# Moving q0's load, the output weights and the first mixer of an attention and token-mixer kernel

## The chip, the cores and the metric

The kernel runs on one core of one Trainium2 chip. The core has five engines with queues of their own: TensorE (PE, whose weight loads are listed as PEld), VectorE (DVE), ScalarE (ACT), GpSimd (POOL) and SyncE (SP). Each executes its instructions in the order of the program and waits where a semaphore says so. The metric is device time in microseconds (us) for one execution; lower is better. The profile is one execution taken by the hardware profiler.

## The reference

There are 4 batches, 8 heads, 768 positions and a head size of 64, in f32. The first half is a causal linear attention with a decay per head; the second mixes the tokens of each batch.

```
for each block of 64 positions:
    intra = (qb @ kb.T * lam**(i - j) for i >= j) @ vb
    inter = (qb * lam**(i + 1)) @ state
    out   = intra + inter
    state = lam**64 * state + (kb * lam**(63 - i)).T @ vb
x  = out as [4, 768, 512]
wq = x @ w_q          # 512 -> 64
wk = x @ w_k
W  = (wq @ wk.T) / 8
y  = relu(W @ x) @ w_out   # 512 -> 512
```

The kernel need not follow the blocks of 64: it uses chunks of 128, and it regroups W @ x as wq @ (wk.T @ x), which needs no matrix of 768 by 768.

## The kernel before, in words

**Tiling.** Two heads make a pair, so that their 2 x 64 columns fill 128 partitions. There are 16 pairs, four a batch, and the main loop has one step for each pair: step n, with n from 0 to 15 (`for n in range(N)`, L553). Lambda's powers are folded into q (`Dq`, multiplied in at L234) and v (`DvI`, multiplied in by `scale_v`, L198), so scores need only a 0/1 mask.

**Loads.** For each pair q, k and v are read as f32 and cast to bf16 on the way, by DMAs that GpSimd issues (`load_q` L81, `load_kv` L86; 196 KB written each). Pair 0 is different: k and q come as f32 by SP (L101, L103) and are cast on chip (L525 to L533). GpSimd's queue holds, in one order, its constants, all these loads, the scaling of v from pair 4 on, and the weights: `wqk` (L190) and `wo`, the 512 by 512 output weights, which step 3 issues (L557). A dictionary `pool` (L545) lists what GpSimd does in steps 0 to 5; from step 6 on `load_more(n + 5)` does.

**One step on PE, in order.** `scores(n)` (12 matmuls), `inter(n-1)`, `values(n-1)`, `flip(n-2)` (transposes of the attention output into `xT`), the outputs of the list `outs`, `turn_q(n+1)` and `turn_k(n+1)` (transposes of the next q and k), `states(n)`, then the outputs of `late_outs`. DVE multiplies the scores by the mask in four pieces a step (`masks`, L320), multiplies the transposed q by Dq, copies `xT` and sums the states; ACT copies k (L252), the attention output (L361) and the output products (L515).

**The mixer of a batch** comes in parts: `mix_wk` (x @ w_k), `mix_wq` (x @ w_q), `mix_py` (wk.T @ x, and its three copies into Y, of which the last two put the halves' partitions the other way round), `mix_pm` (Y with wq, then ReLU into `rmT`; dd numbers the four blocks of 128 columns, each in two halves of 384 positions), and `mix_po` (rmT @ wo for 128 positions, a copy, and a store). In the second half of the kernel one batch's mixer runs within the attention steps of the next. `mix_py` stands at the end of steps 5, 9 and 13, `mix_pm` at the head of steps 7 and 8 (batch 0), 11 and 12 (batch 1), 15 and after the loop.

**What sets the order.** The order is written out by hand; nothing reorders it. [...] Stores wait: at step 9 SP issues a dummy copy (`late`, L573) that waits for the load of v of pair 14, and only then the stores.

Of the kernel before, what the change touches and what calls it, by code (L numbers as in the profile page):

```python
# [10 lines left out]
BF16 = mybir.dt.bfloat16  # L11
F32 = mybir.dt.float32
ALU = mybir.AluOpType
ACT = mybir.ActivationFunctionType

B, H, S, D = 4, 8, 768, 64
CH = 128
# [11 lines left out]
def kernel(  # L29
# [28 lines left out]
    def pst(shape, dt, name):  # L58
        i = free.pop(0)
        t = ps.tile(shape, dt, tag=f"p{i}", name=name)  # L60
        held[id(t)] = (t, i)
        return t

    def done(t):
        free.append(held.pop(id(t))[1])
# [7 lines left out]
    def q_rows(n):  # L73
        b, kk = pairs[n]
        return q[b, 2 * kk : 2 * kk + 2].rearrange("h (a p r) d -> p h a (r d)", p=128, r=2)
# [10 lines left out]
    def load_kv(n, nm):  # L86
        t = stage.tile([128, 2, NCH, D], BF16, tag="f" + nm, name="f" + nm)
        nc.gpsimd.dma_start(out=t, in_=kv_rows(n, dict(k=k, v=v)[nm]))  # L88
        staged[n, nm] = t

    def load(n):
        load_q(n)
        load_kv(n, "k")
        load_kv(n, "v")


    load_kv(0, "v")
    lam1 = consts.tile([1, H], F32, name="lam1")
    nc.sync.dma_start(out=lam1, in_=lam.rearrange("(o h) -> o h", o=1))
    k0 = consts.tile([128, 2, NCH, D], F32, name="k0")  # L100
    nc.sync.dma_start(out=k0, in_=kv_rows(0, k))  # L101
    q0 = consts.tile([128, 2, 3, 2 * D], F32, name="q0")
    nc.sync.dma_start(out=q0, in_=q_rows(0))  # L103


    nc.scalar.preload_act_table_set("natural_log_exp_and_others")
# [3 lines left out]
    nc.vector.memset(blank, 0.0)  # L110
    ident = consts.tile([128, 128], BF16, name="ident")
    nc.vector.memset(ident, 0.0)
    maskc = consts.tile([128, 3, CH], BF16, name="maskc")
    nc.vector.memset(maskc, 1.0)
    nc.gpsimd.affine_select(
# [13 lines left out]
        channel_multiplier=1,  # L129
        allow_small_or_imprecise_dtypes=True,  # L130
    )
    ET = consts.tile([128, S], F32, name="ET")
    nc.gpsimd.iota(
        ET,
        pattern=[[128, NCH], [1, 2], [2, 64]],
        base=1,
        channel_multiplier=0,
        allow_small_or_imprecise_dtypes=True,
    )
    load(1)  # L140
    nc.gpsimd.affine_select(
        out=maskc.rearrange("j c (r p) -> j c r p", r=2),
        in_=maskc.rearrange("j c (r p) -> j c r p", r=2),
# [19 lines left out]
    lnl = consts.tile([128, H], F32, name="lnl")  # L163
    nc.scalar.activation(out=lnl, in_=lam_all, func=ACT.Ln)
    done(lam_all)
    pw48 = consts.tile([128, H, NCH], F32, name="pw48")
    nc.vector.tensor_tensor(
        out=pw48,
# [1 line left out]
        in1=lnl.unsqueeze(2).to_broadcast([128, H, NCH]),  # L170
        op=ALU.mult,
    )
    lnv = lnl.rearrange("p (k l) -> p k l", l=2)
    lncol = consts.tile([128, NP], F32, name="lncol")
    for hl in range(2):
        nc.vector.tensor_copy(
            out=lncol[hl * 64 : hl * 64 + 64, :], in_=lnv[hl * 64 : hl * 64 + 64, :, hl]
        )
    Dq = [consts.tile([128, S], BF16, name=f"dq{kk}") for kk in range(NP)]

    def make_dq(kk):
        nc.scalar.activation(out=Dq[kk], in_=ET, func=ACT.Exp, scale=lncol[:, kk : kk + 1])

    DvI = consts.tile([128, H, NCH], F32, name="DvI")
    nc.scalar.activation(out=DvI, in_=pw48, func=ACT.Exp, scale=-1.0)

    wqk = consts.tile([128, 2, 4, DHY], BF16, name="wqk")
    wo = consts.tile([128, 4, HD], BF16, name="wo")

    def load_wqk():  # L190
        for i, w in ((1, moe_w_k), (0, moe_w_q)):
# [29 lines left out]
    def turn_q(n):  # L221
        b, kk = pairs[n]
        fq = staged.pop((n, "q"))
        trq = pst([128, NCH, 2, 64], BF16, "trq")
        for a in range(3):
            for r in range(2):
                for hl in range(2):
                    nc.tensor.transpose(  # L228
                        trq[hl * 64 : hl * 64 + 64, 2 * a : 2 * a + 2, r, :],
                        fq[:, hl, a, r * D : (r + 1) * D],  # L230
                        ident,
                    )
        qT = tsb.tile([128, S], BF16, tag="qT", name="qT")
        nc.vector.tensor_tensor(  # L234
            out=qT,
            in0=trq.rearrange("d c r p -> d (c r p)"),
            in1=Dq[kk],
            op=ALU.mult,
        )
        done(trq)  # L240
        L[n]["qT"] = qT
# [75 lines left out]
    def masks(n, which):  # L317
        for a, hl in which:
            t = prb.tile([128, 3, CH], BF16, tag="pr", name="pr")
            nc.vector.tensor_tensor(out=t, in0=L[n]["sc"][a, hl], in1=maskc, op=ALU.mult)  # L320
            done(L[n]["sc"][a, hl])
            L[n]["pr"][a, hl] = t
# [175 lines left out]
    def mix_po(b, t, last=False):  # L498
        cols = (256, 256) if last and t == NCH - 1 else (HD,)
        osb = outp.tile([128, HD], F32, tag="osb", name="osb")  # L500
        c = 0
        for w in cols:
            po = pst([128, w], F32, "po")
            for kt in range(4):
                nc.tensor.matmul(  # L505
                    po,
                    M[b]["rmT"][:, kt, t * CH : (t + 1) * CH],
                    wo[:, kt, c : c + w],
                    start=(kt == 0),
                    stop=(kt == 3),  # L510
                )
            if last and (c or (t % 2 and len(cols) == 1)):
                nc.vector.tensor_copy(out=osb[:, c : c + w], in_=po)
            else:
                nc.scalar.copy(out=osb[:, c : c + w], in_=po)  # L515
            done(po)
            stores.append((b, t, c, w, osb))
            c += w
        if b > 0:
            store()  # L520
# [7 lines left out]
    make_dq(0)  # L528
    turn_k(0)
    warm(2)  # L530
    fq0 = nat.tile([128, 2, 3, 2 * D], BF16, tag="q0", name="fq0")
    nc.vector.tensor_copy(out=fq0[:, 0], in_=q0[:, 0])  # L532
    nc.vector.tensor_copy(out=fq0[:, 1], in_=q0[:, 1])  # L533
    staged[0, "q"] = fq0
    turn_q(0)
    warm(2)
    scale_v(0, nc.vector)
# [2 lines left out]
    load_kv(5, "k")  # L540
    load_wqk()
    load_kv(5, "v")


    pool = {  # L545
        0: ["q6", "k6", "s4", "v6"],
        1: ["q7", "k7", "s5", "v7"],
        2: ["q8", "s6", "k8", "v8"],
        3: ["wo"],
        4: ["s7", "q9", "k9"],  # L550
        5: ["s8", "v9", "q10", "k10", "v10"],
    }
    for n in range(N):  # L553
        b, kk = pairs[n]
        for what in pool.get(n, []):
            if what == "wo":
                nc.gpsimd.dma_start(  # L557
                    out=wo, in_=moe_w_out.rearrange("(kt p) j -> p kt j", p=128)
                )
            elif what[0] == "s":  # L560
                scale_v(int(what[1:]), nc.gpsimd)
            elif what[0] == "q":
                load_q(int(what[1:]))
            else:
                load_kv(int(what[1:]), what[0])
        if 11 <= n + 5 < N:
            load_more(n + 5)
        if n + 5 >= N and n + 3 < N:
            scale_v(n + 3, nc.gpsimd)
        if n == 9:  # L570

            late = consts.tile([1, D], BF16, name="late")
            nc.sync.dma_start(out=late, in_=staged[14, "v"][0:1, 0, 0, :])  # L573
            store()
        p = b - 1
        outs = {
            8: [(0, 0), (0, 1)],
            9: [(0, 3)],
            11: [(0, 5)],
            12: [(1, 0)],  # L580
            13: [(1, 2)],
            14: [(1, 3)],
            15: [(1, 5)],
        }.get(n, [])

        late_outs = {8: [(0, 2)], 10: [(0, 4)], 12: [(1, 1)], 14: [(1, 4)]}.get(n, [])

        def back():

            if kk == 1 and n > 8:  # L590
                flip(n - 2, nc.scalar)
            if n >= 1:
                values(n - 1)
            if n >= 2 and not (kk == 1 and n > 8) and n != 5:
                flip(n - 2, nc.scalar if n < 5 else None)
            for i, t in outs:
                mix_po(i, t)
            if kk == 1 and n > 8:
                mix_wk(p)


        if n > 5 and n % 4 in (3, 0):
            mix_pm(
                (n - 5) // 4,
                [0, 1] if n % 4 == 3 else [2, 3],
                engs=(nc.scalar, nc.vector) * 2 if n > 8 else None,
            )
        scores(n)
        if n >= 1:
            inter(n - 1)  # L610
        masks(n, ((0, 0), (0, 1)))
        back()

        if 1 <= n < 3:
            make_dq(n + 1)
        if n in (2, 3):
            scale_v(n, nc.vector)
        masks(n, ((1, 0),))
        if n < N - 1:
            turn_q(n + 1)  # L620
        masks(n, ((1, 1),))
        if n < N - 1:
            turn_k(n + 1)
        states(n)
        if n == 4:
            flip(n - 1)
        for i, t in late_outs:
            mix_po(i, t)
        sums(n)
        if n == 0:  # L630
            scale_v(1, nc.vector)
        if n == 4:
            mix_wk(p, (0, 1, 2))
            mix_wk(p, (3,))
        if n == 5 or kk == 1 and n > 8:
            mix_wq(p)
            mix_py(p)
    bl = B - 1
# [52 lines left out]
```

## Time and profile before

| | us |
|---|---|
| median of 11 runs | 102.16 |
| shortest, longest | 100.14, 105.72 |
| the profiled execution | 105.52 |
| its span, first to last instruction | 103.7 |
| PE busy | 86.0 (83% of the span) |
| DVE, ACT, POOL busy | 68.0, 63.2, 66.0 |
| start of the scores of steps 5 to 9 | 28.23, 32.45, 35.64, 39.34, 51.68 |
| start of the scores of steps 10 to 15 | 57.12, 60.86, 65.38, 70.17, 75.61, 80.21 |

The profiled execution is one of the long ones: 3.4 us above the median of the runs shown. Busy time is the share in which an engine has an instruction in execution; matmuls overlap in a pipeline, so a busy PE is not PE at its best. The timeline lists, for each group of instructions, its start, its length, the engine, the line, what is written and read, and, in brackets, how long the engine was idle just before and what ended that.

### The profile page before, as it was taken

The page shows a single profiled execution, that of the slowest core. Times are in us where ns is not written, and L with a number is a line of the kernel's source. Part 1 is how long each engine was busy: PE and PEld are TensorE (multiplying, and loading weights), DVE is VectorE, ACT ScalarE, POOL GpSimd, SP SyncE. Part 2 cuts the span into 40 slices and gives each one's busy share as a digit, 9 for nine tenths or more (in the row PEclk, how much of TensorE's full clock was granted, in tenths as well). Part 3 has the DMA queues.
Part 4 walks back from the last instruction along what each step waited for, and adds up shares of the span by engine and source line. Part 5 has one row for each costly group of instructions (what it writes and reads, how often), then busy time and mean ns, then how long its engine had stood idle before and what let it go on. Part 6 is the DMA issues. An engine that isn't in the chain of part 4 may idle for free.

```text
span 103.7 us, 3512 instructions
## 1 busy us (share of the span) xinstructions
PE 86.0 (83%) x1497; PEld 57.5 (55%) x1507; DVE 68.0 (66%) x152; ACT 63.2 (61%) x122; POOL 66.0 (64%) x69
## 2 busy tenths in 40 slices
PE   4967678687998998039999999899999989999950
PEld 1415566566887685013778856556966566443430
DVE  3247999797695988300538999995698993246330
ACT  4281487897466989002577876666796775568330
POOL 5999999889989980999999999990500000000000
PEclk9999999999999999855899999999999999999999
DMA  0999999999999999999999999999972221533583
GB/s 20 257 177 156 164 166 165 160 172 154 163 168 163 139 131 159 117 100 151 160 161 150 150 131 154 145 123 299 394 281 103 101 108 58 203 143 132 227 311 140
DMA packets 67440, 16.99 MB, mean 164 GB/s; under 512 B 62946, under 2 KB 64482, under 8 KB 67426
## 3 DMA queue, kind: packets, MB, share of 16 engines
q0 software_dynamic: 61456, 9.70, 127.4%
q1 hardware_dynamic: 5826, 6.95, 18.8%
q8 instruction: 11, 0.18, 0.6%
q10 hardware_dynamic: 144, 0.13, 0.4%
q14 instruction: 3, 0.02, 0.1%
HBM read 20.19 MB, written 6.29 MB: 255 GB/s over the span
## 4 chain that ended last, share of the span: by engine, by line
PE 38%; DMA 25%; POOL 17%; DVE 11%; ACT 3%; issue 3%; POOLq 0%
PE po L505 18%; DMA wo<-in_moe_w_out_dram 11%; DMA fk<-in_k_dram 8%; DMA fv<-in_v_dram 6%; POOL fv L88 5%; POOL fk L88 5%; DVE pr L320 4%; PE trq L228 3%; POOL fq L83 3%; POOL vn L202 3%; PE xp L369 3%; PE oa L349 2%; DVE rmT L477 2%; PE wk L392 2%; PE py L433 2%
## 5 line engine op out<-in xcount | busy, mean ns | idle before, releaser
L320 DVE TENSOR_TENSOR pr<-sc,maskc 128x384 bf16<-128x384 f32 x64 | 33.4, 548 | 2.4 <-PE sc L307 2.1
L505 PE MATMUL po<-wo,rmT 128*128 128x512 bf16 (+1 forms) x90 | 24.4, 390 | 5.0 <-DMA wo<-in_moe_w_out_dram 4.2
L515 ACT COPY osb<-po 128x512 f32<-128x512 f32 (+1 forms) x22 | 12.6, 580 | 15.6 <-PE po L505 15.1
L202 POOL TENSOR_TENSOR vn<-fv,DvI 128x768 bf16<-128x768 bf16 x12 | 17.9, 1492 | 6.0 <-DMA fv<-in_v_dram 3.3
L252 ACT COPY kT<-trk 128x768 bf16<-128x768 bf16 x16 | 12.8, 802 | 8.1 <-PE trk L248 8.1
L88 POOL DMA_DIRECT2D fv<-in_v_dram x16 | 17.1, 1071 | 0.9 <-POOLq L675 0.8
L361 ACT CAST xnat<-oa 128x384 bf16<-128x384 f32 x31 | 13.4, 483 | 6.7 <-PE oa L349 6.6
L505 PEld LDWEIGHTS <-rmT 128*128 128x128 bf16 x100 | 8.9, 101 | 13.9 <-DMA wo<-in_moe_w_out_dram 4.4
L88 POOL DMA_DIRECT2D fk<-in_k_dram x15 | 15.7, 1049 | 0.4 <-DMA fk<-in_k_dram 0.4
L234 DVE TENSOR_TENSOR qT<-trq,dq 128x768 bf16<-128x768 bf16 x16 | 8.8, 552 | 10.7 <-PE trq L228 9.9
L83 POOL DMA_DIRECT2D fq<-in_q_dram x15 | 12.8, 853 | 0.3 <-issue 0.3
L307 PE MATMUL sc<-qT,kT 64*128 64x128 bf16 x192 | 9.5, 217 | 3.5 <-ACT kT L252 2.1
L307 PEld LDWEIGHTS <-kT 64*128 64x128 bf16 x192 | 6.1, 94 | 8.3 <-ACT kT L252 5.3
L228 PE MATMUL trq<-ident,fq 128*64 128x128 bf16 x192 | 9.2, 229 | 1.8 <-DVE fq L532 0.7
L228 PEld LDWEIGHTS <-fq 128*64 128x64 bf16 x192 | 6.3, 113 | 5.5 <-issue 2.9
L486 ACT ACTIVATE rmT<-pm 128x384 bf16<-128x384 f32 x20 | 8.6, 500 | 0.1
L248 PE MATMUL trk<-ident,fk 128*64 128x128 bf16 x180 | 7.8, 223 | 0.7 <-DMA fk<-in_k_dram 0.6
L349 PE MATMUL oa<-vn,pr 128*128 128x64 bf16 x192 | 8.4, 194 | 0.0
L369 PE MATMUL xp<-ident,xnat 128*128 128x128 bf16 x96 | 8.0, 219 | 0.2
L267 PE MATMUL dps<-vn,fk 128*64 128x128 bf16 (+4 forms) x150 | 7.9, 232 | 0.1
L349 PEld LDWEIGHTS <-pr 128*128 128x128 bf16 x192 | 6.6, 98 | 0.7
L267 PEld LDWEIGHTS <-fk 128*64 128x64 bf16 x150 | 6.2, 110 | 1.0 <-DVE xT L377 0.4
(63 smaller groups left out, 111.0 us busy)
## 6 DMA issues: line engine op xcount, KB each, us to landing
out_dram<-osb SPq DMA_DIRECT2D x23, 256.0 KB, 2.1
fv<-in_v_dram POOLq DMA_DIRECT2D x16, 192.0 KB, 6.2
fq<-in_q_dram POOLq DMA_DIRECT2D x15, 192.0 KB, 5.8
fk<-in_k_dram POOLq DMA_DIRECT2D x15, 192.0 KB, 6.2
wo<-in_moe_w_out_dram POOLq DMA_DIRECT2D x1, 512.0 KB, 11.2
k<-in_k_dram SPq DMA_DIRECT2D x1, 384.0 KB, 3.5
q<-in_q_dram SPq DMA_DIRECT2D x1, 384.0 KB, 5.7
out_dram<-osb ACTq DMA_DIRECT2D x1, 128.0 KB, 2.1
```

The costliest lines, as they stand in the source:

```text
L83: nc.gpsimd.dma_start(out=t, in_=q_rows(n))
L88: nc.gpsimd.dma_start(out=t, in_=kv_rows(n, dict(k=k, v=v)[nm]))
L202: eng.tensor_tensor(out=vn, in0=fv, in1=DvI[:, 2 * kk : 2 * kk + 2, :].unsqueeze(3).to_broadcast([128, 2, NCH, D]), op=ALU.mult,)
L228: nc.tensor.transpose(trq[hl * 64 : hl * 64 + 64, 2 * a : 2 * a + 2, r, :], fq[:, hl, a, r * D : (r + 1) * D], ident,)
L252: nc.scalar.copy(out=kT, in_=trk)
L267: nc.tensor.matmul(dps[hl * 64 : hl * 64 + 64, c:end, :], kn[:, hl, c, :], vn[:, hl, c, :].unsqueeze(1).to_broadcast([128, end - c, D]), s ...
L307: nc.tensor.matmul(sc[a, hl][:, cc, :], kT[r, c * CH : (c + 1) * CH], qchunk(n, r, c), start=True, stop=True, skip_group_check=True,)
L320: nc.vector.tensor_tensor(out=t, in0=L[n]["sc"][a, hl], in1=maskc, op=ALU.mult)
L349: nc.tensor.matmul(oa[hl][:, c, :], pr[c // 3, hl][:, c % 3, :], vn[:, hl, c, :], start=False, stop=(c == NCH - 1), skip_group_check=True,)
L361: nc.scalar.copy(out=to, in_=oa[hl])
L505: nc.tensor.matmul(po, M[b]["rmT"][:, kt, t * CH : (t + 1) * CH], wo[:, kt, c : c + w], start=(kt == 0), stop=(kt == 3),)
L515: nc.scalar.copy(out=osb[:, c : c + w], in_=po)
```

## The change

It has five parts. (1) The ramp `ET` is made by a running sum on DVE instead of an iota on GpSimd, in natural order; the Exp that makes Dq reads it with a stride of two elements to get the order it needs. (2) q of pair 0 is loaded by GpSimd as all the others, first in its queue, and q of pair 1 third; SP's f32 load and the two DVE casts go. (3) `wo` is laid out as four blocks of 128 columns, loaded in pieces of 128 columns, and issued behind q and k of pair 6, ahead of the loop; the lists in `pool` are shifted to suit. (4) In step 5 `mix_wq` stands behind `turn_q`, `mix_py` behind `turn_k`, and the first two blocks of `mix_pm` at the end of the step. (5) The other blocks of `mix_pm` come one to a step (`thirds`, at the head of steps 7, 8 and 10 to 15), half by ACT and half by DVE, and the outputs are spread anew over `outs` and `late_outs`.

```diff
@@ -94,13 +94,13 @@
         load_kv(n, "v")
 
 
+    load_q(0)
     load_kv(0, "v")
+    load_q(1)
     lam1 = consts.tile([1, H], F32, name="lam1")
     nc.sync.dma_start(out=lam1, in_=lam.rearrange("(o h) -> o h", o=1))
     k0 = consts.tile([128, 2, NCH, D], F32, name="k0")
     nc.sync.dma_start(out=k0, in_=kv_rows(0, k))
-    q0 = consts.tile([128, 2, 3, 2 * D], F32, name="q0")
-    nc.sync.dma_start(out=q0, in_=q_rows(0))
 
 
     nc.scalar.preload_act_table_set("natural_log_exp_and_others")
@@ -110,6 +110,18 @@
     nc.vector.memset(blank, 0.0)
     ident = consts.tile([128, 128], BF16, name="ident")
     nc.vector.memset(ident, 0.0)
+
+    one = consts.tile([128, 1], F32, name="one")
+    nc.vector.memset(one, 1.0)
+    ET = consts.tile([128, S], F32, name="ET")
+    nc.vector.tensor_tensor_scan(
+        out=ET,
+        data0=one.to_broadcast([128, S]),
+        data1=one.to_broadcast([128, S]),
+        initial=0.0,
+        op0=ALU.mult,
+        op1=ALU.add,
+    )
...
-    ET = consts.tile([128, S], F32, name="ET")
-    nc.gpsimd.iota(
-        ET,
-        pattern=[[128, NCH], [1, 2], [2, 64]],
-        base=1,
-        channel_multiplier=0,
-        allow_small_or_imprecise_dtypes=True,
-    )
-    load(1)
+    load_kv(1, "k")
+    load_kv(1, "v")
...
@@ -163,6 +168,12 @@
     lnl = consts.tile([128, H], F32, name="lnl")
     nc.scalar.activation(out=lnl, in_=lam_all, func=ACT.Ln)
     done(lam_all)
+    lnv = lnl.rearrange("p (k l) -> p k l", l=2)
+    lncol = consts.tile([128, NP], F32, name="lncol")
+    for hl in range(2):
+        nc.vector.tensor_copy(
+            out=lncol[hl * 64 : hl * 64 + 64, :], in_=lnv[hl * 64 : hl * 64 + 64, :, hl]
+        )
...
-    lnv = lnl.rearrange("p (k l) -> p k l", l=2)
-    lncol = consts.tile([128, NP], F32, name="lncol")
-    for hl in range(2):
-        nc.vector.tensor_copy(
-            out=lncol[hl * 64 : hl * 64 + 64, :], in_=lnv[hl * 64 : hl * 64 + 64, :, hl]
+    Dq = [consts.tile([128, S], BF16, name=f"dq{kk}") for kk in range(NP)]
+
+    def make_dq(kk):
+        nc.scalar.activation(
+            out=Dq[kk].rearrange("d (c r p) -> d c r p", c=NCH, r=2),
+            in_=ET.rearrange("d (c p r) -> d c r p", c=NCH, r=2),
+            func=ACT.Exp,
+            scale=lncol[:, kk : kk + 1],
         )
-    Dq = [consts.tile([128, S], BF16, name=f"dq{kk}") for kk in range(NP)]
-
-    def make_dq(kk):
-        nc.scalar.activation(out=Dq[kk], in_=ET, func=ACT.Exp, scale=lncol[:, kk : kk + 1])
 
     DvI = consts.tile([128, H, NCH], F32, name="DvI")
     nc.scalar.activation(out=DvI, in_=pw48, func=ACT.Exp, scale=-1.0)
 
     wqk = consts.tile([128, 2, 4, DHY], BF16, name="wqk")
-    wo = consts.tile([128, 4, HD], BF16, name="wo")
+    wo = consts.tile([128, 4, 4, CH], BF16, name="wo")
 
...
@@ -500,19 +510,21 @@
         osb = outp.tile([128, HD], F32, tag="osb", name="osb")
         c = 0
         for w in cols:
-            po = pst([128, w], F32, "po")
+            po = pst([128, w // CH, CH], F32, "po")
             for kt in range(4):
                 nc.tensor.matmul(
                     po,
                     M[b]["rmT"][:, kt, t * CH : (t + 1) * CH],
-                    wo[:, kt, c : c + w],
+                    wo[:, c // CH : (c + w) // CH, kt, :],
                     start=(kt == 0),
                     stop=(kt == 3),
                 )
             if last and (c or (t % 2 and len(cols) == 1)):
-                nc.vector.tensor_copy(out=osb[:, c : c + w], in_=po)
+                nc.vector.tensor_copy(
+                    out=osb[:, c : c + w], in_=po.rearrange("p a j -> p (a j)")
+                )
             else:
-                nc.scalar.copy(out=osb[:, c : c + w], in_=po)
+                nc.scalar.copy(out=osb[:, c : c + w], in_=po.rearrange("p a j -> p (a j)"))
             done(po)
             stores.append((b, t, c, w, osb))
             c += w
@@ -528,10 +540,6 @@
     make_dq(0)
     turn_k(0)
     warm(2)
-    fq0 = nat.tile([128, 2, 3, 2 * D], BF16, tag="q0", name="fq0")
-    nc.vector.tensor_copy(out=fq0[:, 0], in_=q0[:, 0])
-    nc.vector.tensor_copy(out=fq0[:, 1], in_=q0[:, 1])
-    staged[0, "q"] = fq0
     turn_q(0)
     warm(2)
     scale_v(0, nc.vector)
@@ -540,24 +548,35 @@
     load_kv(5, "k")
     load_wqk()
     load_kv(5, "v")
+    load_q(6)
+    load_kv(6, "k")
+    nc.gpsimd.dma_start(
+        out=wo, in_=moe_w_out.rearrange("(kt p) (a j) -> p a kt j", p=128, j=CH)
+    )
 
 
     pool = {
-        0: ["q6", "k6", "s4", "v6"],
-        1: ["q7", "k7", "s5", "v7"],
-        2: ["q8", "s6", "k8", "v8"],
-        3: ["wo"],
-        4: ["s7", "q9", "k9"],
-        5: ["s8", "v9", "q10", "k10", "v10"],
+        0: ["s4", "v6"],
+        1: ["q7", "s5", "k7", "v7"],
+        2: ["q8", "k8", "s6", "v8"],
+        3: ["q9", "s7", "k9", "v9"],
+        4: ["q10", "s8", "k10", "v10"],
+    }
+
+    thirds = {
+        7: [(0, 2)],
+        8: [(0, 3)],
+        10: [(1, 0)],
+        11: [(1, 1)],
+        12: [(1, 2)],
+        13: [(1, 3)],
+        14: [(2, 0)],
+        15: [(2, 1)],
     }
     for n in range(N):
         b, kk = pairs[n]
         for what in pool.get(n, []):
-            if what == "wo":
-                nc.gpsimd.dma_start(
-                    out=wo, in_=moe_w_out.rearrange("(kt p) j -> p kt j", p=128)
-                )
-            elif what[0] == "s":
+            if what[0] == "s":
                 scale_v(int(what[1:]), nc.gpsimd)
             elif what[0] == "q":
                 load_q(int(what[1:]))
@@ -574,16 +593,22 @@
             store()
         p = b - 1
         outs = {
-            8: [(0, 0), (0, 1)],
-            9: [(0, 3)],
-            11: [(0, 5)],
-            12: [(1, 0)],
-            13: [(1, 2)],
+            8: [(0, 0)],
+            10: [(0, 3)],
+            13: [(1, 0)],
+            14: [(1, 2)],
+            15: [(1, 4)],
+        }.get(n, [])
+
+        late_outs = {
+            8: [(0, 1)],
+            9: [(0, 2)],
+            10: [(0, 4)],
+            12: [(0, 5)],
+            13: [(1, 1)],
             14: [(1, 3)],
             15: [(1, 5)],
         }.get(n, [])
-
-        late_outs = {8: [(0, 2)], 10: [(0, 4)], 12: [(1, 1)], 14: [(1, 4)]}.get(n, [])
 
         def back():
 
@@ -599,12 +624,8 @@
                 mix_wk(p)
 
 
-        if n > 5 and n % 4 in (3, 0):
-            mix_pm(
-                (n - 5) // 4,
-                [0, 1] if n % 4 == 3 else [2, 3],
-                engs=(nc.scalar, nc.vector) * 2 if n > 8 else None,
-            )
+        for i, dd in thirds.get(n, []):
+            mix_pm(i, [dd], engs=(nc.scalar, nc.vector))
         scores(n)
         if n >= 1:
             inter(n - 1)
@@ -618,9 +639,13 @@
         masks(n, ((1, 0),))
         if n < N - 1:
             turn_q(n + 1)
+        if n == 5:
+            mix_wq(p)
         masks(n, ((1, 1),))
         if n < N - 1:
             turn_k(n + 1)
+        if n == 5:
+            mix_py(p)
         states(n)
         if n == 4:
             flip(n - 1)
@@ -632,7 +657,9 @@
         if n == 4:
             mix_wk(p, (0, 1, 2))
             mix_wk(p, (3,))
-        if n == 5 or kk == 1 and n > 8:
+        if n == 5:
+            mix_pm(0, [0, 1], engs=(nc.scalar, nc.vector) * 2)
+        if kk == 1 and n > 8:
             mix_wq(p)
             mix_py(p)
     bl = B - 1
```

More of the change, by code (lines that the diff above doesn't have):

```diff
@@ L542 @@
     load_kv(5, "v")
-    pool = {
-        0: ["q6", "k6", "s4", "v6"],
-        1: ["q7", "k7", "s5", "v7"],
-        2: ["q8", "s6", "k8", "v8"],
-        3: ["wo"],
-        4: ["s7", "q9", "k9"],
-        5: ["s8", "v9", "q10", "k10", "v10"],
+    load_q(6)
+    load_kv(6, "k")
+    nc.gpsimd.dma_start(
+        out=wo, in_=moe_w_out.rearrange("(kt p) (a j) -> p a kt j", p=128, j=CH)
+    )
+    pool = {
+        0: ["s4", "v6"],
[13 more added lines that the diff above has]
+        15: [(2, 1)],
     }
@@ L599, in back @@
                 mix_wk(p)
-        if n > 5 and n % 4 in (3, 0):
-            mix_pm(
-                (n - 5) // 4,
-                [0, 1] if n % 4 == 3 else [2, 3],
-                engs=(nc.scalar, nc.vector) * 2 if n > 8 else None,
-            )
+        for i, dd in thirds.get(n, []):
+            mix_pm(i, [dd], engs=(nc.scalar, nc.vector))
         scores(n)
```

## Prediction

> **What bounds the kernel now.** I read the page first, then the chain of waits, then stretches of the timeline.
>
> The page gives the shape: a dent in the TensorE clock in the middle, and a chain in which waits for DMAs hold a quarter.
>
> ```profile
> PEclk9999999999999999855899999999999999999999
> ...
> PE 38%; DMA 25%; POOL 17%; DVE 11%; ACT 3%; issue 3%; POOLq 0%
> ```
>
> The chain in order of time (start, length, what) shows where the DMA share sits: GpSimd feeds loads, and the last DMA in it is `wo`, issued at 34.33 and landed 11.15 us later. After it the chain is almost all PE.
>
> ```profile
> 13.77 7.82 DMA fk<-in_k_dram
> ...
> 24.33 6.43 DMA fv<-in_v_dram
> ...
> 34.33 11.15 DMA wo<-in_moe_w_out_dram
> ...
> 45.53 0.61 PE po L505
> ```
>
> Three stages follow. **Steps 0 to 4 follow the loads.** In the timeline PE's k transposes wait for their load step after step (start, length, engine, what, idle time before and who ended it):
>
> ```profile
> 10.79 0.53 PE L248 MATMUL trk<-ident,fk 128*64 128x128 bf16 x12 [0.18 <-DMA fk<-in_k_dram]
> ...
> 14.40 0.53 PE L248 MATMUL trk<-ident,fk 128*64 128x128 bf16 x12 [0.36 <-DMA fk<-in_k_dram]
> ```
>
> The spacing is 3.6 us for three loads, so 1.2 us a load (196 KB written, 163 GB/s, which is what the page's GB/s row holds all through). **Step 8 stalls.** Table of stages (us, each engine's busy time, clock, DMA share, GB/s):
>
> ```profile
> 35.60:39.30 3.70, 3.47 (x78) 2.56 (x78) 3.35 (x8) 3.20 (x8) 2.84 (x3) 1.00 1.53 135
> 39.30:51.70 12.40, 7.78 (x87) 4.26 (x90) 4.13 (x9) 4.35 (x9) 10.15 (x10) 0.72 1.68 137
> 51.70:57.10 5.40, 5.26 (x122) 4.38 (x122) 3.25 (x9) 3.97 (x7) 5.40 (x6) 1.00 2.18 156
> ```
>
> Step 8 takes 12.4 us instead of about 4.5 to 5.4: its first output product waits 4.24 us for `wo`, then runs at half clock (eight matmuls from 45.53 to 49.05). **From step 9 on PE is the bound** (5.26 busy of 5.40), save for stretches of DVE in steps 10 to 12. Where the change will cut in, the timeline reads:
>
> ```profile
> 56.37 0.82 PE L433 MATMUL py<-xnat,wkn 128*64 128x256 bf16 x12
> ...
> 57.12 0.51 PE L307 MATMUL sc<-qT,kT 64*128 64x128 bf16 x12
> ...
> 57.23 0.37 ACT L442 CAST Y<-py 128x256 bf16<-128x256 f32 x1
> ...
> 57.61 0.74 ACT L448 CAST Y<-py 64x256 bf16<-64x256 f32 x2
> ```
>
> Today the scores of step 10 start as `py` ends, and the three Y copies (to 58.35) lie beside them.
>
> [...]
>
> **The change, part by part.**
>
> 1. *Scan for ET, reordered constants.* A 128x768 DVE multiply takes 0.95 us (vn, L202)[...] DVE sits idle 2.7 us before pw (waiting for lnl), so it costs 0; were that cover gone, lncol and DvI would slip up to 1 us, with first use in step 0. POOL loses the 0.88 us iota. The Exp with its stride of two: 0.94 us today[...]. I take 0.
> 2. *q0 by GpSimd.* Two DVE casts (0.36 + 0.68) and their wait for q0 (1.4 us) go, one 0.84 us issue is added before v0's, and v0 is later by as much. The scores of step 0 could start at about 8.2 instead of 9.64. But step 1 needs k1, and what must be read before k1 (k0, q0, v0, q1) is the same bytes. [...] I take k1 to k4 0.3 earlier.
> 3. *wo ahead of v6.* It is 512 KB written, 2.67 loads, so 3.2 us at the stream's rate; upper bound, what it took before: v8's scaling waited until 41.48, 10.7 us after v6 landed (30.76) where six loads need 7.2, and wo landed 4.0 after that, so about 3.5 + 4.0, say 7.1 with the hand-over off. It is now 256-byte pieces as q's loads have, so I take 3.2. Its issue (0.78 today, 1.2 guessed for four times the pieces, from 0.84 for 768 and 1.04 for 1536) stands before s4, which ends near 24.7 rather than 24.3: step 4's states need it at about 25, so 0. Everything behind wo in the queue, from v6 on, is later by 3.2: k4 lands at 21.3; v4, q5, k5, two wqk (0.33 each), v5, q6, k6 are 6.67 loads, so k6 29.3, wo 32.5, v6 33.7, k7 36.1, k8 39.7, k9 43.3. Before, k7's successor steps began at 35.64 and 39.34; now step n's scores start 1.5 us after k(n)'s transposes can (37.83 to 39.34 shows the 1.5): step 7 at 37.6, step 8 at 41.2.
> 4. *Mixer within step 5.* wq, py, Y and two pm blocks move from the steps' edges into step 5, which grows to about 5.2 us (27.9 to 33.1, today 4.2), with ACT carrying xnat, wqT, kT, Y and rmT (4.3 us). It is hidden: step 7 waits for k7 anyway. If k7 came 4 us earlier, it would cost about 1.
> 5. *Step 8 without the wait.* From 41.2: pm 0.25, scores 0.44, inter 0.16, values 0.46, flip 0.34, two outputs of 0.86, trq 0.46, trk 0.34, states 0.35 make 4.5, plus 0.2 for the wait for gs: step 9 at 45.9 instead of 51.7. **-5.8.**
> 6. *Outputs.* Two instead of three precede step 9; the third comes after it: **+0.86**. In step 9 no output stands between flip(7) and wk any more: wk waits for ACT's xT copy (0.80 and its hand-over) with only values (0.46) beside part of it: **+0.6** (bounds 0.3 to 0.9).
> 7. *pm right behind py.* In steps 10 and 14 pm (dd 0) now heads PE's queue, and its second half reads the Y half that ACT copies last. PE waits from 57.12 to about 58.4 by the rows above: 1.28 us, with scores, inter, values, outputs and the next transposes queued behind. Twice: **+2.56** (bounds 0.6, if later slack takes it, to 2.8).
> 8. *One block a step.* rmT on DVE is 0.47 once a step instead of twice in steps 11 and 12, where the chain runs through DVE: **-0.4** (bounds 0 to -1).
> 9. *Free:* `wo` read in 128-column blocks by PE, the reshaped po copies: same elements; if a blocked read were slower, po's 17.9% of the chain would tell.
>
> Sum: -5.8 + 0.86 + 0.6 + 2.56 - 0.4 = -2.2, so 105.5 - 2.2 = **103.3 us**. This is against the profiled execution (span 103.7, time 105.52), which is among the longest of what is shown: median 102.16, 100.14 to 105.72. I hold that its excess is the stall itself: with loads at rate, wo would have landed near 41.2 and k9 near 43.6, step 9 begun at 45.4 (two outputs 1.72, trq 0.46, then k9's transposes, states and an output 1.5), and the run taken 105.5 - 6.3 = 99.2, close to the shortest shown. So most runs before lose less than this one, the change has less to give back in them, and its own costs stay. 103.3 is 1.1% above the median. From no change a measurement of this kernel can tell about 1%, so 101.1 to 103.2 counts as within.
>
> **Rivals.**
>
> *Forecast (0.52): stall gone, half of it given back at steps 9, 10 and 14.* 101.8 to 104.8; slower 0.33, within 0.17, faster 0.02.
>
> *wo as slow in its new place (0.18).* If 7.1 us and not 3.2, k7 lands at 40.0 with nothing before it to do from about 35.5; PE idles over 4 us, the clock halves again, and step 9 starts near 50 to 50.5: 103.3 + 4.3 = 107.6. [...] Against it: q's loads of the same pieces land every 3.6 us on time. It decides once wo takes over 5 us. Slower 0.18.
>
> *Not slower: the Y waits are regained (0.26).* Place: steps 11, 12 and 15, where DVE's 3.5 us of masks, qT, sums and xT plus rmT exceed PE's 2.7 to 3.6. If PE reaches those waits early, the 1.28 of step 10 is absorbed, and py to Y shortens at 14: 103.3 - 2.6 = 100.7; and if the profiled run is long all over, not at the stall, the forecast scales to 102.16 x 103.3 / 105.5 = 100.0. It decides when PE idles over 1 us in step 11 behind DVE. For it: DVE in the chain from 58.6 to 66.2. Against: steps 13 and 14 hold five or six microseconds of PE work with no such slack. Faster 0.22, within 0.04.
>
> The remaining 0.04 is split 0.02, 0.01, 0.01. Together: slower 0.53, within 0.22, faster 0.25. Range 99.8 to 106.8: down to the regained case, up to most of the slow-wo case.
>
> **What would show it.** No clock dent and no wait for `wo`; trk waiting for k7 and k8 near 36 and 40; step 9 near 46; pm waiting on ACT's Y copies for about 1.3 us at the head of steps 10 and 14; po at 0.86 per four. I am wrong if wo lands after 35, if step 9 begins after 48, or if those pm waits are under half a microsecond.

## The result, and the profile after

The changed kernel takes 103.82 us (median of 12 runs, 103.35 to 105.24); the kernel before, in 47 runs beside and ahead of them, 102.22 us (100.14 to 105.72). The ratio is 1.029, with a 95% interval of 1.026 to 1.033: slower. The ratio is not the quotient of the two medians, because it leaves out the executions of either kernel that are over 1.5% above its fastest (29 of the 47 of before), and what remains of before lies at about 100.9 us. The profiled execution took 103.66 us, with a span of 101.8.

The page, against that of before: the dent in the clock is gone, and so is `wo` from the chain.

```profile
PEclk9999999999999999999999999999999999999998
...
PE 45%; POOL 22%; DMA 16%; ACT 7%; DVE 4%; issue 2%; POOLq 0%; ACTq 0%
PE po L515 20%; DMA fk<-in_k_dram 8%; DMA fv<-in_v_dram 7%; POOL fv L88 6%; POOL fq L83 6%; POOL fk L88 5%; PE xp L379 3%; PE oa L359 3%; POOL vn L212 3%; PE trq L238 3%; PE trk L258 3%; PE wq L422 2%; PE wk L402 2%; PE py L443 2%; PE dps L277 2%
```

The table of stages, cut near the scores of steps 8 to 14 (us, then the busy time of PE, PE's weight loads, DVE, ACT, POOL, the clock, the DMA share and GB/s), shows what took its place:

```profile
41.40:45.80 4.40, 4.40 (x84) 2.94 (x86) 3.86 (x9) 2.55 (x5) 4.40 (x5) 1.00 1.92 140
45.80:53.40 7.60, 6.16 (x126) 4.53 (x127) 3.56 (x9) 5.29 (x11) 7.60 (x8) 1.00 2.10 151
53.40:58.00 4.60, 4.60 (x87) 3.10 (x89) 4.03 (x10) 2.78 (x6) 4.60 (x5) 1.00 1.91 138
...
65.40:73.60 8.20, 7.18 (x132) 5.04 (x133) 4.60 (x14) 6.19 (x13) 4.66 (x4) 1.00 1.51 265
```

Step 8 takes 4.4 us and PE is never idle in it. But from the scores of step 9 to those of step 10 it is 7.6 us, with 1.4 of them idle on PE, where before had 5.4; from step 13 (65.51) to 14 (73.56) it is 8.05 against 5.4, with 1.0 idle. The line of before for step 13:

```profile
70.20:75.60 5.40, 5.26 (x122) 4.37 (x122) 3.40 (x10) 3.98 (x7) 1.47 (x1) 1.00 1.20 360
```

The rest of the growth is work of PE that stands here now and stood elsewhere in before: the block of pm in both steps, and one output more in step 13. For the idle time the timeline names the cause (the brackets give the idle time and who ended it):

```profile
47.91 0.79 PE L402 MATMUL wk<-wqk,xT 128*128 128x64 bf16 x21 [0.45 <-ACT xT L385]
...
52.60 0.33 PE L476 MATMUL pm<-wqT,Y 64*128 64x384 bf16 x1 [0.47 <-ACT Y L452]
...
53.37 0.33 PE L476 MATMUL pm<-wqT,Y 64*128 64x384 bf16 x1 [0.44 <-ACT Y L458]
53.38 0.55 PE L317 MATMUL sc<-qT,kT 64*128 64x128 bf16 x10
```

wk waits for the copy into xT, and the two matmuls of pm wait for ACT's copies into Y one after the other; the scores of step 10 stand behind them. Step 14 repeats it at 72.79 and 73.56.

In the first half PE now waits for k7 and k8, and `wo` is in long before it is wanted (issued at 22.60, 9.5 us to landing, so 32.1):

```profile
35.96 0.53 PE L258 MATMUL trk<-ident,fk 128*64 128x128 bf16 x12 [0.78 <-DMA fk<-in_k_dram]
...
39.89 0.53 PE L258 MATMUL trk<-ident,fk 128*64 128x128 bf16 x12 [0.55 <-DMA fk<-in_k_dram]
```

```profile
wo<-in_moe_w_out_dram POOLq DMA_DIRECT2D x1, 512.0 KB, 9.5
```

### The profile page after: what moved, and what is told of

Read it like the earlier page. It is cut to its first block, busy times and chain, and to the rows that moved or that the text cites. A ratio compares the mean times of both kernels' runs of the same rounds, so it can differ in the third digit from the quotient of the medians.

```text
span 101.8 us, 3520 instructions
## 1 busy us (share of the span) xinstructions
PE 85.3 (84%) x1507; PEld 57.2 (56%) x1507; DVE 70.8 (70%) x156; ACT 62.0 (61%) x118; POOL 66.7 (65%) x69
## 4 chain that ended last, share of the span: by engine, by line
PE 45%; POOL 22%; DMA 16%; ACT 7%; DVE 4%; issue 2%; POOLq 0%; ACTq 0%
PE po L515 20%; DMA fk<-in_k_dram 8%; DMA fv<-in_v_dram 7%; POOL fv L88 6%; POOL fq L83 6%; POOL fk L88 5%; PE xp L379 3%; PE oa L359 3%; POOL vn L212 3%; PE trq L238 3%; PE trk L258 3%; PE wq L422 2%; PE wk L402 2%; PE py L443 2%; PE dps L277 2%
## 5 line engine op out<-in xcount | busy, mean ns | idle before, releaser
L212 POOL TENSOR_TENSOR vn<-fv,DvI 128x768 bf16<-128x768 bf16 x12 | 18.4, 1530 | 4.4 <-DMA fv<-in_v_dram 4.4
L83 POOL DMA_DIRECT2D fq<-in_q_dram x16 | 14.1, 880 | 0.8 <-POOLq L702 0.8
L487 DVE TENSOR_SCALAR rmT<-pm 128x384 bf16<-128x384 f32 x16 | 8.5, 552 | 6.3 <-PE sc L317 5.0
L317 PE MATMUL sc<-qT,kT 64*128 64x128 bf16 x192 | 8.7, 217 | 3.0 <-ACT kT L262 2.8
L238 PE MATMUL trq<-ident,fq 128*64 128x128 bf16 x192 | 8.6, 223 | 0.0
L476 PE MATMUL pm<-wqT,Y 64*128 64x384 bf16 x32 | 5.8, 331 | 2.3 <-ACT Y L458 1.3
L496 ACT ACTIVATE rmT<-pm 128x384 bf16<-128x384 f32 x16 | 7.5, 496 | 0.1
```

The source lines that it names most:

```text
L83: nc.gpsimd.dma_start(out=t, in_=q_rows(n))
L212: eng.tensor_tensor(out=vn, in0=fv, in1=DvI[:, 2 * kk : 2 * kk + 2, :].unsqueeze(3).to_broadcast([128, 2, NCH, D]), op=ALU.mult,)
L238: nc.tensor.transpose(trq[hl * 64 : hl * 64 + 64, 2 * a : 2 * a + 2, r, :], fq[:, hl, a, r * D : (r + 1) * D], ident,)
L317: nc.tensor.matmul(sc[a, hl][:, cc, :], kT[r, c * CH : (c + 1) * CH], qchunk(n, r, c), start=True, stop=True, skip_group_check=True,)
```

## The experiments

Theory: the stall of step 8 goes for good, but most executions of before lose only one or two microseconds to it; the new order of pm and outputs behind step 9 costs about four. Rivals: `wo` costs in its new place too; the waits for Y are regained by later slack; the first profile of before was long all over. Part 4 of the change (the mixer within step 5) has no run of its own: step 6 began at 32.82, and PE still waited 0.78 us for k7 in it, so no cost of it reaches step 7.

A useful measure below is the *tail*: from the start of step 9's scores to the end of the last output product. It was 99.96 - 51.68 = 48.28 us before and 98.02 - 45.78 = 52.24 us after.

### The kernel before, a second execution

No edit.

> The kernel before, unchanged, for a second look at where its time varies. Theory (the excess of the first profile is the wait for wo in step 8): in a shorter execution, wo lands between 41 and 43 us instead of 45.5, the scores of step 9 start between 45.5 and 48 instead of 51.7, and the stretch from there to the last output product keeps its 48.3 us within 0.3. Rival (the first profile was long all over): step 9 starts near 51 again and the stretch behind it is 2 us or more shorter.

Measured: 100.83 us, span 99.0. Timeline of this execution:

```profile
42.88 1.90 PE L505 MATMUL po<-wo,rmT 128*128 128x512 bf16 x7 [1.31 <-DMA wo<-in_moe_w_out_dram]
...
47.01 0.51 PE L307 MATMUL sc<-qT,kT 64*128 64x128 bf16 x12
```

`wo` landed at 42.8, PE waited 1.31 us instead of 4.24, the clock stayed full (9 in every slice of PEclk), and the first two products took 1.82 us to the transposes behind them (42.88 to 44.70) where the first profile took 3.52 at a granted clock of 0.50: step 9 at 47.0, 4.7 us earlier than in the first profile. The tail is 48.28, the same. So the whole excess of the first profile lay in step 8. Another 59 executions of before fit this when they are sorted by the mean clock each was granted: 101.06 us in the median of 23 at 0.99 or more, 102.81 of 20 at 0.975 to 0.99, 104.03 of 16 below. The clock alone doesn't say in which step an execution lost its time. But the spread goes with `wo`'s old place: those 59 took 100.30 to 106.31 us, while 22 executions of the last version below, which has `wo` ahead and was run beside them, took 100.07 to 101.51. Why the same transfer lands at 42.8 in one execution and at 45.5 in another is not shown.

### `wo` ahead, and nothing else

```diff
+    load_q(6)
+    load_kv(6, "k")
+    nc.gpsimd.dma_start(
+        out=wo, in_=moe_w_out.rearrange("(kt p) (a j) -> p a kt j", p=128, j=CH)
+    )
...
-        0: ["q6", "k6", "s4", "v6"],
+        0: ["s4", "v6"],
...
-        3: ["wo"],
```

(On the kernel before, with the products reading the blocked layout.)

> The kernel before with one part alone: wo in 128-column pieces behind q and k of pair 6, with pm, outputs and pair 0 as before. Theory (wo's new place removes the stall and gates steps 7 and 8 by k7 and k8; what makes the changed kernel slow is the order in steps 9 to 15): step 7 at 37.9, step 8 at 41.5, step 9 at 46.9, time 100.7, level with the shorter runs of before (0.99 to 1.005) and without a dent in the clock. Rival (wo's new place is itself what costs): 103 or more.

Measured: 101.74 us (100.92 to 103.22); 1.0004 of before, 0.986 to 1.015. Steps 7, 8 and 9 began at 37.63, 41.56 and 47.28, with no dent. The stall is gone, and nothing is gained on the executions without a long one: step 7 now waits for k7 (PE idle 0.90 us), and step 9 begins no earlier than in the second execution of before (47.01). The time is 1.0 above what theory said: 0.4 of it is there by step 9 (47.28 for 46.9), 0.4 in the tail (48.7). Still, `wo`'s place is not the main part of what makes the changed kernel slow: the interval, wide with four runs, leaves it at most 1.5% of the 2.9%.

### Pieces or rows

The changed kernel with `wo` in rows of 512 columns:

```diff
-        out=wo, in_=moe_w_out.rearrange("(kt p) (a j) -> p a kt j", p=128, j=CH)
+        out=wo, in_=moe_w_out.rearrange("(kt p) j -> p kt j", p=128)
```

> The changed kernel with wo laid out and loaded as before (rows of 512 columns, 1 KB pieces), in its new place behind q and k of pair 6. Theory (bytes set the landing): wo lands within 0.7 us of 32.1, time within 0.5 us of 103.8. Rival (large pieces land late wherever they stand): wo lands at 35 or later, k7 and k8 later by as much, a dent in the clock, 106 or more.

Measured: `wo` landed at 31.8, 103.53 us, 1.027 of before (1.016 to 1.038). The other way about, the kernel before with 128-column pieces in the old place:

```diff
-                    out=wo, in_=moe_w_out.rearrange("(kt p) j -> p kt j", p=128)
+                    out=wo, in_=moe_w_out.rearrange("(kt p) (a j) -> p a kt j", p=128, j=CH)
```

> The kernel before with wo in 128-column pieces, issued where it was, in step 3. Theory (bytes and place set wo's landing, not the size of the pieces): wo lands between 41 and 45.5 us, time within 0.5% of before, runs as spread as before's. Rival (the 1 KB pieces made stragglers): wo lands before 41.7, step 9 starts by 45.5, time 99.3 to 100.2 and steady.

Measured: 103.01 us (102.0 to 104.18), 1.012 of before (0.997 to 1.028): the time did not stay within half a percent, though the interval holds no change (the plain median of the seven executions of before beside it was 102.4). `wo` landed at 43.2 and PE waited:

```profile
43.27 2.69 PE L505 MATMUL po<-wo,rmT 128*128 128x512 bf16 x8 [2.17 <-DMA wo<-in_moe_w_out_dram]
45.88 0.85 PE L228 MATMUL trq<-ident,fq 128*64 128x128 bf16 x12
```

No effect of the size of the pieces shows in either place: 31.8 and 32.1 in the new one, and 43.2 in the old one lies between the 42.8 and 45.5 of the unchanged kernel. In the new place the landings agree with the prediction's count of the bytes ahead of `wo` in the queue (32.5); in the old place the count gave 41.2, and no execution traced had it before 42.8.

### Pair 0 alone

The kernel before with the first hunks of the change alone (q0 and q1 by GpSimd, scan, strided Exp):

```diff
+    load_q(0)
     load_kv(0, "v")
+    load_q(1)
...
-    q0 = consts.tile([128, 2, 3, 2 * D], F32, name="q0")
-    nc.sync.dma_start(out=q0, in_=q_rows(0))
...
+    nc.vector.tensor_tensor_scan(
```

> The kernel before with pair 0's part alone: q0 first by GpSimd, q1 third, ET by a scan on DVE, the strided Exp. Theory (the loads' bytes set the pace from step 1 on; wo's wait in step 8 moves with the loads): step 0 at 8.3 instead of 9.64, steps 1 to 5 0.3 to 0.9 earlier, wo 0 to 0.5 earlier, time within 0.5% of before. Rival (the whole 1.3 us of the start is kept): 1% faster than before or more.

Measured: step 0 at 8.30, step 1 at 11.55 (0.8 earlier), step 5 at 27.69 (0.5 earlier than in the first profile, 0.3 than in the second); 102.72 us against 102.92, ratio 0.994 (0.987 to 1.002). The 1.3 us of the start shrink to half a microsecond or less, and step 8 still waits 2.3 us for `wo`.

### pm behind the outputs in steps 10 and 14

On the changed kernel:

```diff
+        if n not in (10, 14):
+            pm_block()
         scores(n)
...
         back()
+        if n in (10, 14):
+            pm_block()
```

(`pm_block` is the loop over `thirds`.)

> The changed kernel, but in steps 10 and 14 the pm block stands behind values, flip and outputs instead of at the head of PE's queue. Theory (the two waits for Y cost what they last, about 1 us each): 101.6 to 102.0 against 103.7, PE idle before pm under 0.1 us in both steps. Rival (slack in steps 11, 12 and 15 takes it back): within 0.4 us of the changed kernel.

Measured: 101.65 us (101.5 to 101.8), 1.002 of before (0.992 to 1.012), so 1.9 to 2.2 less than the changed kernel; the tail is 49.92 instead of 52.24. In step 10 scores follow py at once and pm waits for nothing:

```profile
51.81 0.82 PE L443 MATMUL py<-xnat,wkn 128*64 128x256 bf16 x12
52.56 0.51 PE L317 MATMUL sc<-qT,kT 64*128 64x128 bf16 x12
...
54.81 0.34 PE L476 MATMUL pm<-wqT,Y 64*128 64x384 bf16 x2
```

The two waits cost more than the brackets show. These hold 0.91 us a time, 1.82 together, and the tail lost 2.32. The rest is that the two matmuls of pm ran apart, each with a wait ahead: 0.33 us each, where together they take 0.34. The rival that later slack regains the waits falls.

### An output back between values and wk in step 9

Besides the last edit:

```diff
             8: [(0, 0)],
+            9: [(0, 2)],
             10: [(0, 3)],
...
-            9: [(0, 2)],
             10: [(0, 4)],
```

> The changed kernel with pm of steps 10 and 14 behind the outputs (as in the run before this one) and, besides, output (0, 2) back between values and wk in step 9. Theory (without an output there, wk waits 0.45 us for ACT's copy into xT): 101.65 less 0.4 to 0.6, so 101.1 to 101.3. Rival (ACT's copy of that output stands before the copies that wk and values need, and takes the gain back): within 0.15 of 101.65.

Measured: 100.77 us (20 runs), 0.997 of before (0.993 to 1.000). The tail is 49.08, 0.84 less. The wait was 0.45 us, but nearly twice that comes back. With the output in between, wk no longer runs in two parts behind the copy: in parts it took 0.25 and 0.79 us, in one 0.86. That is 0.2 of the rest; the other 0.2 is not taken apart.

```profile
47.29 1.03 PE L515 MATMUL po<-wo,rmT 128*128 128x512 bf16 x4
48.15 0.86 PE L402 MATMUL wk<-wqk,xT 128*128 128x64 bf16 x24
```

### Blocks of pm one by one or in pairs

From the kernel just described, pm of batches 1 and 2 put back to where before had it:

```diff
-        10: [(1, 0)],
-        11: [(1, 1)],
-        12: [(1, 2)],
-        13: [(1, 3)],
-        14: [(2, 0)],
-        15: [(2, 1)],
+        11: [(1, 0), (1, 1)],
+        12: [(1, 2), (1, 3)],
+        15: [(2, 0), (2, 1)],
```

> The kernel with pm behind the outputs and output (0, 2) back in step 9, but with pm of batches 1 and 2 in pairs of blocks at the head of steps 11, 12 and 15, where the kernel before has them. It prices the relief of DVE by one block a step, which the prediction took at 0.4 us. Theory (no relief: PE, not DVE, ends most of these steps): within 0.25 us of its neighbour in this call. Rival (relief as predicted): 0.4 us or more slower.

> The neighbour for the run before it, unchanged from its first run: 100.8 within 0.5 us.

Measured on the same chip, 22 runs each: in pairs 101.35 us, 1.001 of before (0.998 to 1.004); one by one 100.88, 0.997 (0.993 to 1.000). The difference is 0.47 us, and the tails differ by the same (49.59 against 49.08 of the first run). My theory for this run, no relief, falls; the relief that the prediction took at 0.4 is real. The two intervals against before touch, but the two kernels ran beside each other, and the medians of their 22 spans (99.4 and 98.95) lie apart by the same amount. (The profiled execution of the repeated kernel had a wait for loads in step 3 and a dent behind it, 103.13 us, and is not used for the tail.)

With pairs, DVE is busy nearly all through steps 11 and 12 (this kernel's table of stages, cut at the scores of steps 11, 12 and 13; then the same two steps in before, from the first profile):

```profile
56.00:59.60 3.60, 3.26 (x80) 2.38 (x76) 3.54 (x8) 2.79 (x7) 3.60 (x4) 1.00 1.91 144
59.60:64.00 4.40, 3.90 (x78) 2.64 (x78) 4.40 (x12) 2.42 (x5) 4.40 (x5) 1.00 1.91 136
```

```profile
60.90:65.40 4.50, 3.97 (x85) 2.69 (x84) 4.31 (x11) 3.42 (x8) 4.50 (x5) 1.00 1.97 144
65.40:70.20 4.80, 4.59 (x83) 2.92 (x86) 4.61 (x13) 2.95 (x6) 4.62 (x4) 1.00 1.92 135
```

These two steps take 8.05 us with one output in them; the kernel before took 9.31 for the same pm and three outputs (1.72 us of PE more). So two outputs taken out of these steps save 1.26, not 1.72, and cost their full 0.86 each where they go. The next version has the same pm and two outputs here, and tells the two apart.

### A version that uses the room in steps 6 and 7

Loads, pair 0, `wo` and step 5 of the changed kernel; pm of batch 0 done by step 6; outputs from step 7; batches 1 and 2 as before:

```diff
+        6: [(0, 3)],
+        11: [(1, 0), (1, 1)],
+        12: [(1, 2), (1, 3)],
+        15: [(2, 0), (2, 1)],
...
+            7: [(0, 0)],
+            8: [(0, 2)],
+            9: [(0, 4)],
...
+            7: [(0, 1)],
+            8: [(0, 3)],
+            10: [(0, 5)],
...
+            mix_pm(0, [2])
```

(The first group is `thirds`, the second `outs`, the third `late_outs`; those of batch 1 are as before. The block of step 6 stands behind `back()` and goes to ACT alone, as does the added `mix_pm(0, [2])` at the end of step 5.)

> A mix of both: loads, pair 0, wo and step 5 of the changed kernel; all pm blocks of batch 0 done by step 6 (the third by ACT at the end of step 5, the fourth by ACT within step 6), outputs (0, 0) and (0, 1) in step 7, (0, 2) and (0, 3) in step 8, (0, 4) in step 9, (0, 5) in step 10, and pm and outputs of batches 1 and 2 where the kernel before has them. Theory (PE's idle time in steps 6 and 7, about 2 us behind k7 and k8, is free room for outputs): step 9 at 46.2 with four outputs behind it, then 47.4 us to the last output product, time 99.0 to 99.5, and steady. Rival (the outputs in step 7 push k's transposes and copies back one for one): step 9 at 47 or later, 100.3 or more.

Measured: 100.33 us (20 runs, 99.94 to 101.25), 0.995 of before (0.991 to 0.999), and not 99.0 to 99.5. Repeated:

> The neighbour for the run before it, unchanged from its first run: 100.3 within 0.5 us, 0.3 to 0.7% below the undisturbed runs of before.

100.35 us (22 runs), 0.995 (0.992 to 0.998), where the median of before was 102.70. Step 9 began at 46.4 with four outputs done, so the room was real; the tail was 48.0, 0.6 more than expected. It has one output less in it than before's tail and is only 0.29 shorter, and all of that lies in steps 11 and 12 (the repeated run, cut at the scores of steps 11, 12 and 13):

```profile
55.60:59.30 3.70, 3.38 (x83) 2.43 (x78) 3.70 (x10) 2.89 (x7) 3.70 (x4) 1.00 1.85 140
59.30:64.60 5.30, 4.74 (x82) 2.91 (x82) 5.11 (x15) 2.93 (x6) 5.30 (x6) 1.00 1.98 140
```

They take 9.03 us between their scores, where before took 9.31: step 11, without its output, is 0.9 shorter, and step 12, with the same work as in before, 0.6 longer. So the output of step 11 had cost 0.3 us and not 0.86; the one of step 12, by the 8.05 above, cost its full price.

To see what ends step 12, half of DVE's ReLU in steps 11 and 12 went to ACT:

```diff
-                mix_pm(i, [dd], engs=(nc.scalar, nc.vector))
+                a = dd % 2 and n in (11, 12)
+                mix_pm(i, [dd], engs=(nc.scalar, nc.scalar if a else nc.vector))
```

> The kernel with outputs from step 7, but in steps 11 and 12 the DVE half of every second pm block goes to ACT. Theory (DVE ends step 12, where PE waited about 1 us behind masks and ReLU): 0.4 to 0.6 us faster than its neighbour in this call, step 12 at most 4.9 us. Rival (ACT's copies then wait): no change or slower.

Measured: 100.35 us (6 runs), the same as its neighbour; its own ratio, 0.987 (0.981 to 0.993), rests on other executions of before. Step 12 took 5.26 us. The theory falls: DVE's busy time in steps 11 and 12 fell by 0.7 and the steps shortened by 0.1. The timeline of this run shows two short waits at the head of step 12, and none behind them until the scores of step 13 (65.03):

```profile
59.77 0.65 PE L317 MATMUL sc<-qT,kT 64*128 64x128 bf16 x7 [0.26 <-ACT kT L262]
...
60.67 0.34 PE L317 MATMUL sc<-qT,kT 64*128 64x128 bf16 x5 [0.25 <-DVE gs L298]
```

So PE has work for nearly the whole step, and behind another engine it waits half a microsecond, not the one microsecond that the theory took. With step 11 short of its output, PE comes to these scores early and waits for kT and gs; in before, with the output in step 11, only the wait for kT stood there (0.26 us).

## Why the prediction was right or wrong

The sum for the profiled execution held: 103.3 said, 103.66 measured. The direction, slower, held. What failed is the size of it: 1.1% said, 2.9% measured.

**The step that failed is the level it was held against.** The prediction argued that before's first profile was long because of step 8, and that a run at rate would take 99.2; then it compared 103.3 with the median of 102.16. That median mixes executions that lose much in step 8 with some that lose little. The runs show the mechanism right (the tails of the first and the second profile are the same) and its size off: before without a long stall is at about 100.9 (100.83 in the second execution), and not at 99.2, since `wo` lands at 42.8 even then, not 41.2, and step 9 starts at 47.0, not 45.4. (By its own terms, k9 at 43.6 and 1.5 us, the prediction should have had 45.1.) Against 100.9 its 103.3 would have been 2.4%; against its own 99.2, which it worked out and then did not use, 4.1%. A sum made on one long execution gives the new kernel's time, not its distance from the old one.

Point by point:

1. *Scan and constants, 0.* The scan took 1.76 us, where the multiply had taken 0.95, and was hidden; the strided Exp 0.99 against 0.94. Right.
2. *q0, 0.3 earlier.* Steps 1 to 4 began 0.7 to 0.8 earlier, step 5 0.4. The direction was right, the size, the author's estimate, about half of what was measured, and by itself it is worth nothing measurable (0.987 to 1.002).
3. *`wo` at 3.2 us of queue, landing 32.5.* 32.1; k7's transposes 35.96 (36.1), k8's 39.89 (39.7). Pricing by bytes, 1.2 us for each 196 KB written, was the author's estimate from the spacing of the loads; for this place it was right within 0.4 us, and the rival of a slow `wo` (0.18) did not come. What limits the loads was not shown. The issue of `wo` took 1.48 us, not 1.2.
4. *Step 5.* Step 6 began at 32.82 (33.1). Right.
5. *Step 9 at 45.9.* 45.78. Right: -5.9 for -5.8.
6. *Outputs, 0.86 + 0.6.* The second term measured 0.84 when undone. The first is the length of an output in the trace; no run undoes it alone.
7. *Waits for Y, 2.56.* 2.3 in the tail, 1.9 to 2.2 in the time, when undone. Right.
8. *Relief of DVE, -0.4.* 0.5 when undone. Right.
9. *Blocked reads, 0.* The run with rows differed by 0.3 us, in the range of its runs. Right.

Behind step 9 the forecast was +3.6 and the tail grew by 3.96. The terms as measured, 0.86 + 0.84 + 2.32 - 0.5, leave 0.44, which the prediction did not have at all: of the two outputs taken out of steps 11 and 12, the one in step 11 had cost only 0.3 us there. That the sum came within 0.4 us is in part luck: this missing term and the second term of point 6, 0.24 too small, were offset in part by point 7, taken 0.24 too high, and by 0.1 each in points 5 and 8.

The rival "not slower" (0.26) rested on two things. That the profiled run was long all over is refuted by the second execution; that the waits for Y would be regained is refuted by moving pm.

## What to carry to other kernels

Before a sum made on one profile is turned into a ratio, find the stall that varies from run to run, and hold the new time against the old kernel without it. Removing a stall that costs a typical run one or two microseconds doesn't pay for two new waits on the bounding engine, 1.2 us each, that every run has; here they came from moving a consumer to the head of the queue right behind its producer's copies. Filler work is cheapest where the bounding engine would otherwise wait for another: the output in step 11 cost 0.3 us instead of 0.86.

## What was not expected of the hardware

The prediction had the half clock only behind a wait of over 4 us (4.24 in step 8). The traces show it after less. Read in stretches of 0.1 us, the clock of the first profile fell from 1.00 to 0.50 at 43.2, when PE had been idle for 1.9 us, and came back at 50.1, 6.8 us later; 4.5 of these lay behind the wait of 4.24. Three other traces have a dent (pieces in the old place, pair 0 alone, and the repeated kernel with one output back):

```profile
PEclk9999999999999999975999999999999999999999
...
PEclk9999999999999999966999999999999999999999
...
PEclk9999999955799999999999999999999999999999
```

In the first two PE waited 2.2 and 2.3 us for `wo`, was at work again for 1.0 and 0.7 us, and only then the clock fell, for 3.4 us. In the third it waited 2.5 us for a load in step 3, and the half clock lasted 6.8 us. The wait of 1.31 us for `wo` in the second execution of before left the clock full. So waits of 2.5 and 4.24 us were followed by the same 6.8 us of half clock, and the shortest of these waits that had a dent behind it was 2.17 us; what sets the length of the dent is not shown.

The dent of 3.4 us came with another 1.5 us: with the pieces in the old place, the stretch from the first output product to the scores of step 9 took 5.6 us, where the second execution of before took 4.1 at full clock; the 12 transposes of q in it took 0.85 us instead of 0.53.
